# Moving seven weight slots to four addresses modulo 256 in a local-attention and SiLU-FFN kernel

## The chip, the cores and the metric

The kernel runs on one core of one Trainium2 chip. The metric is device time in microseconds (us) of one execution, here the median of three runs. The engines are TensorE (matmuls, PE in the profile; its weight loads are PEld), VectorE (DVE), ScalarE (ACT), GpSimd (POOL), and SyncE (SP), which issues most DMA transfers. SBUF is the on-chip memory with 128 partitions; a tile stands at the same byte address in each partition. PSUM holds the matmuls' sums.

## The reference

A layer norm is followed by two branches on the same normalized input, which are multiplied: dilated local attention with 32 heads of 20, and a SiLU feed-forward network (FFN).

```python
# x: [1, 2048, 640]; wqkv: [640, 1920]; wo: [640, 640]; w1: [640, 1536]; w2: [1536, 640]; all float32
xn = layernorm(x)
q, k, v = split(xn @ wqkv)                        # 32 heads of 20
idx = pos - 2 * arange(8)                         # each position sees 8 earlier ones, 2 apart
attn = softmax(where(idx >= 0, q . k[idx] * 20**-0.5, -1e9))
s = (attn . v[idx]) @ wo
g = silu(silu(xn @ w1) @ w2)
return x + s * g
```

## The kernel before

**Tiling.** The 2048 rows are worked on in four groups of 512 (two halves by two parities of position), and a group in four tiles of 128 rows. For each group there are three kinds of dense work on TensorE, in this order: `qkv_phase` (20 weight units: 4 quarters of the heads by 5 chunks of 128 input channels), from the second group on `wo_phase` for the group before (5 units), and `ffn_phase` (12 units of `w1` and 12 of `w2`, alternating). After the last group `wo_last` closes. Attention itself (scores, softmax, values) runs on VectorE and ScalarE beside the matmuls of the next quarters.

**Three products for one.** Every float32 operand is split into a high and a low half (type float32r), and a product is hi·hi + lo·hi + hi·lo. The activations' halves, transposed, are the tiles `TH[i]` and `TL[i]` (names th and tl in the profile; i is 0 or 1, by group in turn). The hidden layer's halves are `SH[s]` and `SL[s]` (sh and sl; s is the parity of the FFN unit f). A weight unit stands in one of seven ring slots `WR[0]` to `WR[6]` (name w), 5120 bytes per partition: the high half in the first 2560 bytes, the low half in the next. Units take the slots in turn, and a slot is refilled when its unit is done.

**Which operand stands and which moves.** A matmul has a stationary operand, loaded into the array ahead (PEld, 128 columns, 512 bytes per partition), and a moving one that streams through.

| lines | work | stationary | moving | columns | matmuls |
|---|---|---|---|---|---|
| L590 to L592 | qkv | th, tl | w | 480 | 900 |
| L741 to L743 | w1 | w | th, tl | 512 | 720 |
| L624, L626 with sh, sl | w2 | sh, sl | w | 384 and 256 | 576 pairs |
| L624, L626 with th, tl | wo | th, tl | w | 384 and 256 | 240 L624, 225 L626 |
| L542 | first quarter of qkv | th, tl | w | 480 | 60 |

The matmuls of a unit are three per tile and chunk, so on L590 to L592 and on L741 to L743 a block of one unit is 12 and 15 matmuls; on L624 and L626 a `w2` unit is 12 pairs. The order of TensorE's work is written out by hand; a small planner (`Weave`) orders the other engines' work around it by costs and due times. It sees tiles by name, not by address.

**Addresses.** All tiles come from one pool and stand in the order in which the program makes them, rounded up to 32 bytes. All offsets within th, tl, sh, sl and w that the matmuls use are multiples of 256 bytes, so that one number modulo 256 describes each tile.

Of the kernel before, what the change touches and what calls it, by code (L numbers as in the profile page):

```python
# [8 lines left out]
F32 = mybir.dt.float32  # L9
F32R = mybir.dt.float32r  # L10
# [4 lines left out]
P = 128  # L15
S, D, F, H, DH = 2048, 640, 1536, 32, 20
W = 8
DC, FC = D // P, F // P
NQ = 4
HQ = H // NQ  # L20
CQ = HQ * DH
J = 8
T = 4
TOK = T * P
# [5 lines left out]
RING = 7  # L30
# [13 lines left out]
def tsl(t):  # L44
    return slice(t * P, (t + 1) * P)
# [119 lines left out]
def local_attention_silu_ffn(ctx: ExitStack, tc: tile.TileContext, x, wqkv, wo, w1, w2, out):  # L165
    nc = tc.nc
    pool = lambda name, bufs, **kw: ctx.enter_context(tc.tile_pool(name=name, bufs=bufs, **kw))
    sb = pool("sb", 1)
# [16 lines left out]
    def tiles(name, n, shape, dtype=F32):  # L185
        return [sb.tile(shape, dtype, name=f"{name}{i}") for i in range(n)]
# [2 lines left out]
    epst = sb.tile([P, 1], F32, name="epst")  # L189
    MV = sb.tile([P, T, 2], F32, name="mv")  # L190
    ST = [sb.tile([P, 2, 6], F32, name="st0")]
    TH = tiles("th", 2, [P, DC, TOK], F32R)
    TL = tiles("tl", 2, [P, DC, TOK], F32R)
    WR = tiles("w", RING, [P, 2 * D], F32R)
    SH = [None, sb.tile([P, TOK], F32R, name="sh1")]
    SL = [None, sb.tile([P, TOK], F32R, name="sl1")]
    ST.append(sb.tile([P, 2, 6], F32, name="st1"))
    SH[0] = sb.tile([P, TOK], F32R, name="sh0")
    SL[0] = sb.tile([P, TOK], F32R, name="sl0")
    SD = sb.tile([P, 2, T], F32, name="sd")  # L200
    mask = sb.tile([P, T, W], F32, name="mask")
    M = tiles("m", 2, [P, T, HQ])
    Z = tiles("z", 2, [P, 2, T, HQ])
    KV = tiles("kv", NQ, [P, 2, HALO + T, CQ])
    Q = tiles("q", NQ, [P, T, CQ])
# [34 lines left out]
    def dve(n, fn, reads, writes, prio, lock=False):  # L240
        add("DVE", dv(n), fn, reads, writes, prio, lock)

    def act(n, fn, reads, writes, prio, table=None):
        add("ACT", ac(n), fn, reads, writes, prio, table=table)

    def pe(dur, fn, reads, writes):
        add("PE", dur, fn, reads, writes)
        clock[0] += dur
# [44 lines left out]
    for u in units:  # L293
        n = seen[u] = seen.get(u, 0) + 1
# [6 lines left out]
    def width(u):  # L301
        return 3 * CQ if u[0] == "q" else D
# [31 lines left out]
    def w_load():  # L334
# [5 lines left out]
        n = width(u)  # L340
        r = WR[s]
        both = r.rearrange("p (s d) -> p s d", s=2)[:, :, :n]
# [26 lines left out]
    def w_next(*want):  # L369
# [4 lines left out]
        s, n = i % RING, width(want)  # L374
        return WR[s][:, :n], WR[s][:, D:D + n], ("wh", s), ("wl", s)

    def w_done(n=1):
        for _ in range(n):
            w_load()
# [26 lines left out]
    def split_t(src, skeys, c, i):  # L406
# [6 lines left out]
        pe(0.54, turn, skeys, [kp])  # L413
        hi, lo = TH[i][:, c, :], TL[i][:, c, :]
        kh, kl = t_keys(i, [c], kinds=["th"]), t_keys(i, [c], kinds=["tl"])
# [34 lines left out]
    def halo_keys(q):  # L450
        return [("halo", q, 1, 0), ("halo", q, 1, 112), ("halo", q, 2, 0), ("halo", q, 2, 112), ("halo", q, 3, 0),
                ("halo", q, 4, 0)] + [("kv", q, t) for t in range(T)]

    def scores(g, q):
        i = q % 2
        l, e, m, kv, qq = L[i], E[i], M[i], KV[q], Q[q]
        hk = halo_keys(q)
# [51 lines left out]
    def first_quarter(i):  # L509
# [8 lines left out]
        def turn(t):  # L518
# [6 lines left out]
            for a, b, tp, kp in parts:  # L525
                v = tp[:, :(b - a) * P].rearrange("p (c n) -> p c n", n=P)
                act((b - a) * P, lambda a=a, b=b, v=v: nc.scalar.activation(TH[i][:, a:b, tsl(t)], v, AF.Copy),
                    [kp], t_keys(i, range(a, b), [t], ["th"]), 0)
            for a, b, tp, kp in parts:
                v = tp[:, :(b - a) * P].rearrange("p (c n) -> p c n", n=P)  # L530
                dve((b - a) * P, lambda a=a, b=b, v=v: nc.vector.tensor_tensor(
                    out=TL[i][:, a:b, tsl(t)], in0=v, in1=TH[i][:, a:b, tsl(t)].bitcast(F32), op=OP.subtract),
                    [kp] + t_keys(i, range(a, b), [t], ["th"]), t_keys(i, range(a, b), [t], ["tl"]), 0)

        def products(t, part):
            o, kp = ps[t]
            for k in part:
                for c in range(DC):
                    x, kx = (TL, "tl") if k == 1 else (TH, "th")
                    wh, wl, kh, kl = ws[c]  # L540
# [35 lines left out]
    def qkv_phase(g, i, io):  # L576
        for q in range(NQ):
            if g == 0 and q == 0:
                ps = first_quarter(i)
            else:  # L580
                ps = [bank() for t in range(T)]
                for c in range(DC):
                    wh, wl, kh, kl = w_next("q", q, c)
                    for t in range(T):
                        o, kp = ps[t]

                        def unit(c=c, t=t, o=o, wh=wh, wl=wl):
                            o = o[:, :3 * CQ]
                            hi, lo = TH[i][:, c, tsl(t)], TL[i][:, c, tsl(t)]
                            nc.tensor.matmul(o, hi, wh, start=c == 0, stop=False)  # L590
# [17 lines left out]
    def t_keys(i, cs, ts=range(T), kinds=("th", "tl")):  # L608
        return [(k, i, c, t) for k in kinds for c in cs for t in ts]
# [10 lines left out]
    def tm_mm(banks, t, st, w, first, last, cols=(0, 1)):  # L620
        a, b = banks
        h = t % 2
        if 0 in cols:
            nc.tensor.matmul(a[t][0][:, :CA], st, w[:, :CA], start=first, stop=last)  # L624
        if 1 in cols:
            nc.tensor.matmul(b[t // 2][0][:, h * CB:(h + 1) * CB], st, w[:, CA:], start=first and h == 0,  # L626
                             stop=last, skip_group_check=True)
# [14 lines left out]
    def wo_phase(g, i):  # L642
        banks = tm_banks()
        a, b = banks
        for c in range(DC):
            wh, wl, kh, kl = w_next("wo", c)
            for t in range(T):
                def one(c=c, t=t, wh=wh, wl=wl):
                    tm_mm(banks, t, TH[i][:, c, tsl(t)], wh, c == 0, False)
                    tm_mm(banks, t, TH[i][:, c, tsl(t)], wl, False, False)  # L650
                    tm_mm(banks, t, TL[i][:, c, tsl(t)], wh, False, c == DC - 1)
                pe(3 * TM, one, t_keys(i, [c], [t]) + [kh, kl], [a[t][1], b[t // 2][1]])
# [14 lines left out]
    def wo_last(g, i):  # L667
# [22 lines left out]
        def whole(t, cols):  # L690
            for k in range(3):
                for c in range(DC):
                    st = (TH, TH, TL)[k][i][:, c, tsl(t)]
                    tm_mm(banks, t, st, ws[c][k == 1], k + c == 0, k == 2 and c == DC - 1, cols)
# [23 lines left out]
    def ffn_phase(g, i, ix, io):  # L718
        nxt = g + 1 if g + 1 < NG else None
        ps = prev = None  # L720
        for f in range(FC + 1):
# [11 lines left out]
            if f < FC:  # L733
# [11 lines left out]
                w_done()  # L745
                sf, sh, sl = SF[s], SH[s], SL[s]
                act(TOK, lambda sh=sh, h=h: nc.scalar.activation(sh, h, AF.Silu), [kp], [("sh", s)], 0, "silu")  # L747
# [76 lines left out]
```

## Time and profile before

| | |
|---|---|
| three runs | 643.94, 643.47, 643.81 us; median 643.81 |
| the profiled execution's own time | 644.53 us |
| its span, first to last instruction | 642.8 us |
| TensorE busy | 635.4 us, 99% |
| weight loads (PEld) busy | 576.0 us, 90% |
| VectorE, ScalarE, GpSimd busy | 83%, 32%, 20% |
| matmuls | 3502 |

Matmuls overlap in the pipeline and their ends are modelled, so a matmul's duration in the profile says little. What it costs is the time from its start to the start of the next one, which the timeline shows; I call this the spacing.

### The profile page before, as it was taken

Reading aid. Unit: us, or ns where it says so; the run is one execution under the profiler, and the core shown is the slowest. Engines: PE = TensorE matmul, PEld = TensorE weight load, DVE = VectorE, ACT = ScalarE, POOL = GpSimd, SP = SyncE. Lnnn points to the kernel's source line nnn. Section 1 sums busy time; section 2 is a strip of 40 time slices with the busy share of each in tenths; the row PEclk is TensorE's granted clock in tenths of the full one; section 3 lists DMA queues with packets and bytes.
Section 4 is the critical chain, followed back from the end, with each engine's and each line's share of the span. In section 5 each row is a group of like instructions: output and inputs, shape, how many; then the busy total and the mean of one; then the engine's idle time right before and its main releaser. Section 6 shows DMA issues by size and latency. Waiting matters only on the chain.

```text
span 642.8 us, 9033 instructions
## 1 busy us (share of the span) xinstructions
PE 635.4 (99%) x3502; PEld 576.0 (90%) x3502; DVE 536.6 (83%) x532; ACT 206.1 (32%) x401; POOL 126.5 (20%) x171
## 2 busy tenths in 40 slices
PE   7999999999999999999999999999999999999997
PEld 7888899999888999999888999999988899899997
DVE  5699999999999989999939999999106999999714
ACT  5435453453534022324332212223313222233130
POOL 7410000011101241112222125111122213311100
PEclk8999999999999999999999999999999999999999
DMA  9999999777999997656699978965579996876522
GB/s 275 323 309 323 311 403 395 275 226 217 301 319 328 291 306 266 176 184 207 184 257 279 301 215 255 319 180 169 167 203 259 278 293 227 298 258 197 172 83 82
DMA packets 74010, 162.44 MB, mean 253 GB/s; under 512 B 5632, under 2 KB 46816, under 8 KB 73968
## 3 DMA queue, kind: packets, MB, share of 16 engines
q0 software_dynamic: 26672, 82.58, 44.1%
q1 hardware_dynamic: 47296, 79.29, 40.1%
q8 instruction: 27, 0.44, 0.3%
q14 instruction: 15, 0.12, 0.1%
HBM read 109.55 MB, written 34.16 MB: 224 GB/s over the span
## 4 chain that ended last, share of the span: by engine, by line
PE 98%; DMA 1%; DVE 0%; ACT 0%; SPq 0%; issue 0%
PE acc L624 22%; PE acc L626 15%; PE acc L590 10%; PE acc L592 10%; PE acc L591 10%; PE rot L742 9%; PE rot L743 9%; PE rot L741 9%; PE rot L412 2%; PE acc L542 2%; DMA pr<-in_A_wqkv_dram 1%; PE rot L523 0%; PE rot L713 0%; PE acc L515 0%; DVE xin L402 0%; ACT w L355 0%
## 5 line engine op out<-in xcount | busy, mean ns | idle before, releaser
L624 PE MATMUL acc<-w,sh 128*128 128x384 f32 x384 | 114.9, 337 | 0.0
L590 PE MATMUL acc<-w,th 128*128 128x480 f32 x300 | 114.7, 382 | 0.0
L592 PE MATMUL acc<-w,th 128*128 128x480 f32 x300 | 113.5, 378 | 0.0
L591 PE MATMUL acc<-w,tl 128*128 128x480 f32 x300 | 113.4, 378 | 0.0
L626 PE MATMUL acc<-w,sh 128*128 128x256 f32 x384 | 107.2, 279 | 0.0
L460 DVE TENSOR_TENSOR pr<-q,kv 128x2560 f32<-128x2560 f32 x32 | 90.2, 2820 | 11.4 <-DMA kv<-kv 10.9
L741 PE MATMUL rot<-th,w 128*128 128x512 f32 x240 | 94.9, 395 | 0.0
L743 PE MATMUL rot<-th,w 128*128 128x512 f32 x240 | 93.7, 391 | 0.0
L742 PE MATMUL rot<-tl,w 128*128 128x512 f32 x240 | 93.7, 390 | 0.0
L492 DVE TENSOR_TENSOR pr<-e,kv 128x2560 f32<-128x2560 f32 x32 | 90.3, 2821 | 0.7
L463 DVE TENSOR_REDUCE l<-pr 128x128 f32<-128x2560 f32 x32 | 90.0, 2812 | 0.2
L347 POOL DMA_DIRECT2D w<-half_q x52 | 37.5, 721 | 234.3 <-DMA raw<-in_A_wqkv_dram 93.2
L747 ACT ACTIVATE sh<-rot 128x512 fp32r<-128x512 f32 x48 | 28.8, 599 | 159.4 <-PE rot L743 159.3
L497 DVE TENSOR_TENSOR pr<-pr 128x1280 f32<-128x1280 f32 x64 | 76.5, 1195 | 1.1
L347 POOL DMA_DIRECT2D w<-half_w x72 | 38.5, 535 | 181.9 <-PE acc L626 99.2
L626 PEld LDWEIGHTS acc<-w,sh 128*128 128x128 f32 x384 | 72.2, 188 | 1.5
L624 PEld LDWEIGHTS acc<-w,sh 128*128 128x128 f32 x384 | 72.1, 188 | 1.6
L592 PEld LDWEIGHTS acc<-w,th 128*128 128x128 f32 x300 | 56.3, 188 | 8.8
L590 PEld LDWEIGHTS acc<-w,th 128*128 128x128 f32 x300 | 56.3, 188 | 8.3
L591 PEld LDWEIGHTS acc<-w,tl 128*128 128x128 f32 x300 | 56.3, 188 | 8.2
L624 PE MATMUL acc<-w,sl 128*128 128x384 f32 x192 | 58.5, 336 | 0.0
L417 DVE TENSOR_TENSOR tl<-rot,th 128x512 fp32r<-128x512 f32 x35 | 23.9, 682 | 36.4 <-ACT th L416 36.3
(84 smaller groups left out, 1004.8 us busy)
## 6 DMA issues: line engine op xcount, KB each, us to landing
w<-half_w POOLq DMA_DIRECT2D x72, 640.0 KB, 5.6
w<-half_q POOLq DMA_DIRECT2D x52, 480.0 KB, 4.9
half_w<-w SPq DMA_DIRECT2D x24, 640.0 KB
half_q<-w SPq DMA_DIRECT2D x20, 480.0 KB
w<-half_wo POOLq DMA_DIRECT2D x15, 640.0 KB, 4.4
kv<-kv SPq DMA_DIRECT2D x16, 560.0 KB
kv<-kv SPq DMA_DIRECT2D x16, 420.0 KB
gate<-in_B_w_dram SPq DMA_DIRECT2D x16, 320.0 KB
```

What stands on the lines that cost most here:

```text
L460: dve(2560, lambda t=t: nc.vector.tensor_tensor(out=PR, in0=win(qq[:, t:t + 2, :], W, 0), in1=win(kv[:, 0, t:t + 2, :], W, CQ), op=OP.mult ...
L463: dve(2560, lambda t=t: nc.vector.tensor_reduce(out=l[:, t:t + 2].rearrange("p t w h -> p (t w h)"), in_=PR.rearrange("p t w (h d) -> p (t ...
L492: dve(2560, lambda t=t, v=v: nc.vector.tensor_tensor(out=PR.rearrange("p t w (h d) -> p t (w h) d", d=DH), in0=e[:, t:t + 2].rearrange("p ...
L497: dve(2 * n * CQ, lambda n=n: nc.vector.tensor_tensor(out=PR[:, :, 0:n, :], in0=PR[:, :, 0:n, :], in1=PR[:, :, n:2 * n, :], op=OP.add), [] ...
L590: nc.tensor.matmul(o, hi, wh, start=c == 0, stop=False)
L591: nc.tensor.matmul(o, lo, wh, start=False, stop=False)
L592: nc.tensor.matmul(o, hi, wl, start=False, stop=c == DC - 1)
L624: nc.tensor.matmul(a[t][0][:, :CA], st, w[:, :CA], start=first, stop=last)
L626: nc.tensor.matmul(b[t // 2][0][:, h * CB:(h + 1) * CB], st, w[:, CA:], start=first and h == 0, stop=last, skip_group_check=True)
L741: nc.tensor.matmul(h, wh[:, cs], TH[i][:, c, :], start=c == 0, stop=False)
L742: nc.tensor.matmul(h, wh[:, cs], TL[i][:, c, :], start=False, stop=False)
L743: nc.tensor.matmul(h, wl[:, cs], TH[i][:, c, :], start=False, stop=c == DC - 1)
```

## The change

Only the order of the tiles in SBUF changes, and two unused tiles of 64 bytes are added. In the built program the instructions, their order on each engine, their shapes and their waits' order are the same; the addresses differ. Modulo 256 the tiles that TensorE reads stand at:

| tile | before | after |
|---|---|---|
| th0, th1 | 0, 0 | 0, 0 |
| tl0, tl1 | 0, 0 | 0, 128 |
| w0, w1, w2, w3, w4, w5, w6 | 0, 0, 0, 0, 0, 0, 0 | 0, 64, 128, 192, 192, 64, 64 |
| sh0, sl0 | 64, 64 | 64, 64 |
| sh1, sl1 | 0, 0 | 64, 64 |
| ident (transposes) | 128 | 128 |
| xin, o (transposes) | 224, 224 | 96, 96 |

All tiles made after `sd` (z, kv, q, o, pr, l, e, xin, gate, xr, sf, raw) move by the same 128 bytes.

```diff
-    TH = tiles("th", 2, [P, DC, TOK], F32R)
-    TL = tiles("tl", 2, [P, DC, TOK], F32R)
-    WR = tiles("w", RING, [P, 2 * D], F32R)
-    SH = [None, sb.tile([P, TOK], F32R, name="sh1")]
-    SL = [None, sb.tile([P, TOK], F32R, name="sl1")]
-    ST.append(sb.tile([P, 2, 6], F32, name="st1"))
-    SH[0] = sb.tile([P, TOK], F32R, name="sh0")
-    SL[0] = sb.tile([P, TOK], F32R, name="sl0")
+    def apart(n):
+
+        sb.tile([P, n], F32, name=f"apart{len(gaps)}")
+        gaps.append(n)
+
+    gaps = []
+    TH = [sb.tile([P, DC, TOK], F32R, name="th0"), None]
+    TL = [sb.tile([P, DC, TOK], F32R, name="tl0"), None]
+    TH[1] = sb.tile([P, DC, TOK], F32R, name="th1")
+    mask = sb.tile([P, T, W], F32, name="mask")
+    TL[1] = sb.tile([P, DC, TOK], F32R, name="tl1")
+    M = [sb.tile([P, T, HQ], F32, name="m0")]
+    WR = []
+    for k in range(RING):
+        if k == 1:
+            ST.append(sb.tile([P, 2, 6], F32, name="st1"))
+        elif k in (2, 3):
+            apart(16)
+        elif k == 5:
+            M.append(sb.tile([P, T, HQ], F32, name="m1"))
+        WR.append(sb.tile([P, 2 * D], F32R, name=f"w{k}"))
+    SH = tiles("sh", 2, [P, TOK], F32R)
+    SL = tiles("sl", 2, [P, TOK], F32R)
     SD = sb.tile([P, 2, T], F32, name="sd")
-    mask = sb.tile([P, T, W], F32, name="mask")
-    M = tiles("m", 2, [P, T, HQ])
     Z = tiles("z", 2, [P, 2, T, HQ])
```

## The prediction

> **What bounds the kernel.** I read the page first (busy times, granted clock, the chain that ended last), then TensorE's own waits, then the groups by line.
>
> ```profile
> span 642.8 us, 9033 instructions
> ...
> PE 635.4 (99%) x3502; PEld 576.0 (90%) x3502; DVE 536.6 (83%) x532; ACT 206.1 (32%) x401; POOL 126.5 (20%) x171
> ...
> PEclk8999999999999999999999999999999999999999
> ...
> PE 98%; DMA 1%; DVE 0%; ACT 0%; SPq 0%; issue 0%
> ```
>
> ```profile
> PE rot L523 <- DVE xin L402: 2.3, 1, 2.3
> PE rot L515 <- POOL ident masks.py:199: 1.4, 1, 1.4
> ```
>
> The chain that ended last is TensorE for 98% of the span, at full granted clock after the first slice, and TensorE's matmuls wait for others only twice, 3.7 us together, both in the first stage. So the time is the sum of the matmuls' spacings. Any nanosecond that the addresses add to or take from a spacing goes straight into the time; what they do to VectorE, ScalarE or a transfer counts only if TensorE would begin to wait.
>
> The groups give the counts. L591 and L592 have the count of L590, L742 and L743 that of L741.
>
> ```profile
> L624 PE MATMUL acc<-w,sh 128*128 128x384 f32 x384 | 114.9, 337 | 0.0
> L590 PE MATMUL acc<-w,th 128*128 128x480 f32 x300 | 114.7, 382 | 0.0
> L741 PE MATMUL rot<-th,w 128*128 128x512 f32 x240 | 94.9, 395 | 0.0
> L624 PE MATMUL acc<-w,sl 128*128 128x384 f32 x192 | 58.5, 336 | 0.0
> L624 PE MATMUL acc<-w,th 128*128 128x384 f32 x160 | 48.9, 338 | 0.0
> L624 PE MATMUL acc<-w,tl 128*128 128x384 f32 x80 | 25.8, 338 | 0.0
> ```
>
> The spacings come from TensorE's timeline (start, modelled duration, line). Five rows bound four blocks in a row; left out between them are the other matmuls of each block.
>
> ```profile
> 95.72 0.39 PE L741 MATMUL rot<-th,w 128*128 128x512 f32 x1
> ...
> 99.12 0.34 PE L624 MATMUL acc<-w,sh 128*128 128x384 f32 x1
> ...
> 100.28 0.33 PE L624 MATMUL acc<-w,sh 128*128 128x384 f32 x1
> ...
> 102.57 0.40 PE L741 MATMUL rot<-th,w 128*128 128x512 f32 x1
> ...
> 106.02 0.33 PE L624 MATMUL acc<-w,sh 128*128 128x384 f32 x1
> ...
> 109.54 0.60 PE L412 MATMUL rot<-ident,xin 128*128 128x128 f32 x4
> ```
>
> Call the stationary tile's address minus the moving tile's, modulo 256, the distance. The w1 block from 95.72 has 15 matmuls at distance 0: 3.40 us, 226.7 ns each, or 0.4427 ns per column. This is the lowest steady pace I find, and I take it as the pace without stalls. At that pace a pair of 384 and 256 columns takes 283.3 ns and a matmul of 480 columns 212.5 ns.
>
> The w2 block from 99.12 is of sh0 and sl0, at distance 64: 12 pairs in 3.45 us, 287.5 ns each, and from 100.28 on 8 pairs in 2.29 us, 286.2 ns each. The block from 106.02 is of sh1 and sl1, at distance 0: 12 pairs in 3.52 us, 293.3 ns. The two blocks differ in nothing else that the program fixes, so the old layout already holds a trial of the change: distance 64 is worth 5.8 to 7.1 ns per pair. The Trainium skill (TensorE: Matmul & The Clock Gate, Part 2, step on LDWEIGHTS) says the opposite, that loading the next weights takes no read bandwidth from the running matmul; by it these blocks would be alike and the sum of the change nothing. The trace disagrees by those 5.8 ns, in this kernel.
>
> The same rows hold the price. The w1 block after the sh0 block takes 106.02 - 102.57 = 3.45 us, 230.0 ns per matmul, against 226.7 in the block that follows an sh1 block. After a block at another distance the streams need some matmuls to settle; that costs 50 ns per entry here.
>
> The two remaining kinds of work, qkv and wo, all at distance 0:
>
> ```profile
> 56.00 0.38 PE L592 MATMUL acc<-w,th 128*128 128x480 f32 x1
> ...
> 59.90 0.38 PE L592 MATMUL acc<-w,th 128*128 128x480 f32 x1
> ```
>
> ```profile
> 204.45 0.34 PE L624 MATMUL acc<-w,th 128*128 128x384 f32 x1
> ...
> 211.80 0.34 PE L624 MATMUL acc<-w,tl 128*128 128x384 f32 x1
> ```
>
> The first two rows are 18 matmuls apart: 3.90 us, 216.7 ns each, 4.2 over the pace without stalls. The other two are 25 pairs apart: 7.35 us, 294.0 ns, 10.7 over it.
>
> **The change part by part.** Nothing is added or removed on any engine and no wait changes; only distances do. Going through the program's matmuls with the new addresses gives the counts below.
>
> *qkv, 900 matmuls, all at distance 0 now.* After, 132 stay there (w0 with th0, th1 and tl0; w2 with tl1), 280 come to 64, 132 to 128, 356 to 192. Of wo's stall of 10.7 ns per pair, 286.2 - 283.3 = 2.9 ns remain at distance 64, which is 27%. No row shows distances 128 and 192, or 480 columns at any but 0. If 27% of 4.2 ns remain, the gain is 3.0 ns for each of 768: -2.3 us. Bounds: all of the stall goes, -3.2 us; or one more stall of the same size comes in its place, +3.2 us. I take -2.3, from the only row with another distance.
>
> *wo, 240 pairs (15 of them, of the last tile, lack the 256-column half).* All but 4 leave distance 0. At 294.0 - 286.2 = 7.8 ns for 236 pairs that is -1.8 us; bounds -2.5 us (pace without stalls) and 0.
>
> *w2, 576 pairs.* Half stand at distance 0 now, the sh1 blocks. After, sh and sl are all at 64, and so are w1, w5 and w6, which serve half of the w2 units: 288 pairs at distance 0 again, and 96, 144 and 48 at 64, 128 and 192. So this part moves its stalls without removing them. The 192 pairs at 128 and 192 have no row: between 0 and 5.8 ns each more than at 64, 0 to +1.1 us. I take +0.3.
>
> *w1, 720 matmuls.* They run without steady stalls now, so here the change can only cost. 600 leave distance 0. If w1 gets qkv's stall there, 4.2 ns each, that is +2.5 us; if the streams settle into a pace without stalls as they do now, nothing. What is sure to change is the entries: 24 of the 48 blocks follow an sh0 block now. I take half of the other 24 to pay 50 ns: +0.6 us.
>
> *Entries to qkv and wo units.* Each unit is in another slot, and so mostly at another distance than the one before: 75 qkv units after the first quarter and 20 units of wo in the loops. At 50 ns each this is +4.75 us, at none 0. In the trace a change of distance is paid by w1 blocks, while the sh0 block itself, entered from w1, averages only 1.3 ns per pair over its later pace, 16 ns in all. I take 10 ns each: +0.95 us, as some neighbours share a distance.
>
> *Everything else.* The weights are moved by DMA into slots that now start at 64 or 192. A load has much time:
>
> ```profile
> w<-half_w POOLq DMA_DIRECT2D x72, 640.0 KB, 5.6
> ```
>
> ```profile
> 309.95 0.71 POOL L347 DMA_DIRECT2D w<-half_q  x1 [1.89 <-PE acc L592]
> ...
> 325.55 0.71 POOL L347 DMA_DIRECT2D w<-half_q  x1 [1.89 <-PE acc L592]
> ```
>
> These issues are six apart, one per slot that comes free every 2.60 us, and the slot is read again six units later, so 5.6 us stand against some 15. A load would have to take nearly three times as long before TensorE waits; then each us beyond that is lost on each unit. The tiles of VectorE and ScalarE move by the same 128 bytes among themselves, and both have idle time. I cost both at nothing. The first quarter's 60 matmuls on L542 I leave as they are.
>
> *Sum.* -2.3 - 1.8 + 0.3 + 0.6 + 0.95 = -2.25 us. The profiled execution took 644.53 us (1.7 of it around its span), so 642.3; it lies 0.7 us above the median of the runs, 643.81, and on that scale the forecast is 641.6 us.
>
> **The rivals.** *Slower: entries eat the gain.* If every change of slot costs what w1 pays after sh0, 50 ns, then 95 entries of qkv and wo and 24 of w1 cost 5.95 us, and with w2's 1.1 against the gains of 4.1 the time is 643.81 + 2.95 = 646.8 us. It decides from (4.1 - 0.3) / 119 = 32 ns per entry. For it speaks that qkv units last only 12 matmuls, fewer than the block of 15 in which w1 paid; against it the cheap entry into the sh0 block.
>
> *No change worth measuring.* Either the sh0 and sh1 blocks differ for another reason than the distance, which is the skill's rule at work, and the time stays at 643.8; or gains and entries cancel. The alternation of the blocks with sh's parity speaks against the first.
>
> *Full relief.* Only distance 0 stalls, and entries cost nothing: -3.2 for qkv, -2.5 for wo, and w2's 288 other pairs lose their 2.9 ns, -0.8: 643.81 - 6.5 = 637.3 us. Against it: distance 64 did not free the sh0 block fully.
>
> **How the numbers follow.** A measurement of this kernel can tell about 0.2%, 1.3 us, from no change. Forecast (a partial gain between 1.3 and 4.5 us): 0.40. Full relief, or near it: 0.14. No change within 1.3 us: 0.20. Slower: 0.26, all of it from costs without a row (128 and 192, and w1 off distance 0). So faster 0.54, same 0.20, slower 0.26. The likeliest case's own range is 639.3 to 642.5 us. The range that should hold 8 times in 10 goes on one side to near full relief, 637.8, and on the other to near the slower rival, 646.2.
>
> **What would show it.** In the profile after: qkv spacings of 213 to 215 ns in units of w1, w3 to w6, and 216.7 still in w0; wo pairs near 287 ns; w2 blocks near 293 ns in w1, w5 and w6 and near 287 in w0, whatever sh's parity; w1 spacings of 226.7 ns late in each block with longer ones early. Wrong would be: qkv staying at 216.7 at distances other than 0 (then its stall is not one of addresses), w1 blocks that stay above 230 ns throughout, or new waits of PE for DMA.

## The result and the profile after

The changed kernel takes 648.05 us (median of four runs, 647.77 to 648.38) against 643.78 us for the kernel before (643.47 to 643.94), a ratio of 1.0067 with a 95% interval of 1.005 to 1.0085. It is slower by 4.3 us. The forecast was 641.6 us: the sign was wrong, and the time lies 1.9 us above the range.

The page of the kernel after, its span, busy times, granted clock and chain:

```profile
span 646.6 us, 9033 instructions
...
PE 639.1 (99%) x3502; PEld 576.4 (89%) x3502; DVE 539.5 (83%) x532; ACT 206.0 (32%) x401; POOL 125.6 (19%) x171
...
PEclk9999999999999999999999999999999999999999
...
PE 92%; DMA 3%; DVE 2%; ACT 1%; SPq 1%; issue 1%; ACTq 0%
...
w<-half_w POOLq DMA_DIRECT2D x72, 640.0 KB, 5.5
```

TensorE's own waits in the kernel after:

```profile
PE rot L536 <- DVE xin L415: 1.5, 1, 1.5
PE rot L528 <- POOL ident masks.py:199: 1.4, 1, 1.4
PE acc L555 <- ACT w L368: 0.5, 1, 0.5
PE acc L639 <- ACT q L439: 0.3, 1, 0.3
```

The instruction counts and the landing time of the weights (5.5 us, before 5.6) have not moved; the granted clock differs only in the first of the 40 slices (9 tenths, before 8), and TensorE waits 3.7 us for others, as before. The chain has only 92% of TensorE in it because it leaves TensorE at the last of these waits, 0.3 us long; nothing more hangs on that. So the added 3.8 us of span are in the spacings of matmuls that wait for nobody. The groups by line (13 lines further down than before) show it faintly, since a modelled duration carries only part of a spacing:

```profile
L637 PE MATMUL acc<-w,sh 128*128 128x384 f32 x384 | 115.6, 338 | 0.0
L603 PE MATMUL acc<-w,th 128*128 128x480 f32 x300 | 115.2, 384 | 0.0
L754 PE MATMUL rot<-th,w 128*128 128x512 f32 x240 | 95.7, 399 | 0.0
```

For the spacings themselves I took the starts of all 3502 matmuls of both traces in program order and summed the differences by kind. After minus before, in us: qkv +0.59 without its first 100 matmuls, w1 +2.13, w2 +1.25, wo +0.44, the first 100 matmuls of qkv (the first quarter's 60 and the next 40) +0.59, the transposes -1.16 (most of it the wait for `xin`, 2.3 us before and 1.5 now). That is +3.84 us, the whole difference of the spans, 3.8. The last two terms are the start of the program, where a new wait for `w` (0.5 us) and the clock of the first slice play in; I read nothing about addresses from them. No kind of the steady work gained anything.

The timeline of the kernel after (start, modelled duration, line). Each pair of rows bounds one block; left out are the other matmuls of the block:

```profile
67.73 0.39 PE L754 MATMUL rot<-th,w 128*128 128x512 f32 x1
...
71.14 0.33 PE L637 MATMUL acc<-w,sh 128*128 128x384 f32 x1
...
88.72 0.40 PE L754 MATMUL rot<-th,w 128*128 128x512 f32 x1
...
92.22 0.34 PE L637 MATMUL acc<-w,sh 128*128 128x384 f32 x1
...
95.82 0.40 PE L754 MATMUL rot<-th,w 128*128 128x512 f32 x1
...
143.48 0.34 PE L637 MATMUL acc<-w,sh 128*128 128x384 f32 x1
...
146.93 0.34 PE L637 MATMUL acc<-w,sh 128*128 128x384 f32 x1
```

The first block is of w1 units in slot w0, at distance 0: 15 matmuls in 3.41 us, 227.3 ns each, about as before (226.7). The second is in w6, at distance 64: 3.50 us, 233.3 ns. The third and the fourth are w2 units, both of slot w0 at distance 64. One takes 3.60 us for 12 pairs, 300.0 ns; the other 3.45 us, 287.5 ns. Same slot, same distance, and two paces. The two read sh1 and sh0, but that is not it: over the four groups of the program the w2 block of slot w0 with sh1 takes 300, 287, 300 and 287 ns per pair. The two at 287 are in the groups that read th1 and tl1; tl1 stands at 128, so the w1 block just ahead of them has other distances in it. And two neighbouring qkv units, in w2 at distance 128 and then in w3 at distance 64:

```profile
53.78 0.38 PE L603 MATMUL acc<-w,th 128*128 128x480 f32 x1
...
56.42 0.38 PE L603 MATMUL acc<-w,th 128*128 128x480 f32 x1
...
59.02 0.38 PE L603 MATMUL acc<-w,th 128*128 128x480 f32 x1
```

They take 2.64 and 2.60 us for 12 matmuls: 220.0 and 216.7 ns, where distance 0 had 216.7. Distance 64 helps qkv by no more than these rows can show, whose starts are given to 10 ns.

### The profile page after: what moved, and what is told of

It reads as the page before. It is cut to its first block, busy times and chain, and to the rows that moved or that the text cites. A ratio compares the mean times of both kernels' runs of the same rounds, so it can differ in the third digit from the quotient of the medians.

```text
span 646.6 us, 9033 instructions
## 1 busy us (share of the span) xinstructions
PE 639.1 (99%) x3502; PEld 576.4 (89%) x3502; DVE 539.5 (83%) x532; ACT 206.0 (32%) x401; POOL 125.6 (19%) x171
## 4 chain that ended last, share of the span: by engine, by line
PE 92%; DMA 3%; DVE 2%; ACT 1%; SPq 1%; issue 1%; ACTq 0%
PE acc L637 22%; PE acc L639 15%; PE rot L756 9%; PE rot L754 9%; PE rot L755 9%; PE acc L603 8%; PE acc L605 8%; PE acc L604 8%; PE rot L425 2%; PE acc L555 2%; DMA raw<-in_A_wo_dram 2%; DVE pr L505 1%; DMA xin<-in_A_x_dram 1%; SPq L450 1%; DVE pr L510 0%
## 5 line engine op out<-in xcount | busy, mean ns | idle before, releaser
L473 DVE TENSOR_TENSOR pr<-q,kv 128x2560 f32<-128x2560 f32 x32 | 91.6, 2864 | 11.0 <-DMA kv<-kv 10.6
L510 DVE TENSOR_TENSOR pr<-pr 128x1280 f32<-128x1280 f32 x64 | 77.9, 1217 | 1.1
```

The source lines that it names most:

```text
L473: dve(2560, lambda t=t: nc.vector.tensor_tensor(out=PR, in0=win(qq[:, t:t + 2, :], W, 0), in1=win(kv[:, 0, t:t + 2, :], W, CQ), op=OP.mult ...
L510: dve(2 * n * CQ, lambda n=n: nc.vector.tensor_tensor(out=PR[:, :, 0:n, :], in0=PR[:, :, 0:n, :], in1=PR[:, :, n:2 * n, :], op=OP.add), [] ...
```

## The experiments

Three theories stood at the start. The first is the prediction's slower rival: each change of distance, from slot to slot or into a w1 block, costs a time of its own. The second: the distances that the slots were moved to are slower in themselves, for as long as a block lasts. The third: the tiles behind `sd`, which moved by 128 bytes, disturb VectorE, ScalarE or a transfer. Each kernel differs from the kernel before in addresses alone, by the order of the tiles and by unused gaps, unless it is told otherwise. Times are medians, ratios stand against the kernel before on the same chip, and changes by kind are sums of spacings of the profiled execution against the profile before. They leave out the transposes and the first 100 matmuls of qkv, which move by up to 1.8 us from profile to profile.

**sh and sl all at distance 64.** The part of the change that the old trace had a row for, alone:

```diff
-    SH = [None, sb.tile([P, TOK], F32R, name="sh1")]
-    SL = [None, sb.tile([P, TOK], F32R, name="sl1")]
     ST.append(sb.tile([P, 2, 6], F32, name="st1"))
-    SH[0] = sb.tile([P, TOK], F32R, name="sh0")
-    SL[0] = sb.tile([P, TOK], F32R, name="sl0")
+    SH = tiles("sh", 2, [P, TOK], F32R)
+    SL = tiles("sl", 2, [P, TOK], F32R)
```

> Layout of before, with sh1 and sl1 moved to 64 beside sh0 and sl0; th, tl and w stay at 0. So every w2 pair stands at distance 64 and nothing else changes. Theory D (the spacing of a matmul follows from its own distance, whatever came before): the 288 pairs of sh1 go from 293.3 to 286.5 ns, -1.9 us, about 641.9. Theory E (a change of distance between blocks costs an entry): the same gain, but the 24 w1 blocks that followed an sh1 block now pay 50 ns each as well, +1.2 us, about 643.1; w1 spacings then average 230 ns in all 48 blocks. Theory M (TensorE's operands do not matter; the loss came from the tiles that were moved beside them): 643.8, nothing but sh1 and sl1 has moved.

Measured: 643.32 against 643.96 us, ratio 0.9988 (0.9978 to 0.9997). w2 gains 1.2 us and w1 pays 0.53 us. A w1 block behind one of the moved sh1 blocks:

```profile
81.29 0.40 PE L739 MATMUL rot<-th,w 128*128 128x512 f32 x1
...
84.74 0.34 PE L622 MATMUL acc<-w,sh 128*128 128x384 f32 x1
```

It takes 3.45 us. By the unrounded starts such blocks go from 226.9 to 229.7 ns per matmul, 42 ns each. That happens in nine blocks, not in 24: the first two w1 blocks of a group have no w2 block just ahead of them, and those in the stretches with transposes move by 21 ns at most. Away from the transposes, both prices read from the old trace held for this shape and this distance.

**All slots at 64,** sh and sl at 128, so that w1 and w2 stand at 64 and qkv and wo at 192, and no slot differs from another:

```diff
-    WR = tiles("w", RING, [P, 2 * D], F32R)
...
     ST.append(sb.tile([P, 2, 6], F32, name="st1"))
...
+    WR = tiles("w", RING, [P, 2 * D], F32R)
+    sb.tile([P, 16], F32, name="gap6")
+    SH = tiles("sh", 2, [P, TOK], F32R)
+    SL = tiles("sl", 2, [P, TOK], F32R)
+    sb.tile([P, 48], F32, name="gap7")
```

> All seven w slots at 64, all of sh and sl at 128, th and tl at 0, the other tiles where before has them. Distances are the same in every unit: w1 64, qkv and wo 192, w2 64. In the changed kernel w1 at 64 had 232.7 ns and qkv at 192 had 218.2 ns. Theory D: the same here, w1 +4.6 ns x 720 = +3.3 us, qkv +1.4 x 860 = +1.2 us, w2 -1.9 us as all pairs stand at 64: about 646.4. Theory E: with one distance for each kind the streams settle; w1 near 227 to 230 ns, qkv at 216.7, w2 287: 642 to 643. Theory M: 643.8.

Measured: 653.23 against 643.96 us, ratio 1.0145 (1.013 to 1.016): w1 +3.59, w2 +4.4, qkv +1.33, wo -0.1 us. It is the slowest kernel of all, though it has no change of distance between slots; the theory of entries cannot explain it. Its timeline, a w1 block and the w2 block behind it, and in the latter two pairs of 384 and 256 columns:

```profile
82.02 0.40 PE L741 MATMUL rot<-th,w 128*128 128x512 f32 x1
...
85.52 0.34 PE L624 MATMUL acc<-w,sh 128*128 128x384 f32 x1
...
87.31 0.34 PE L624 MATMUL acc<-w,sh 128*128 128x384 f32 x1
87.49 0.28 PE L626 MATMUL acc<-w,sh 128*128 128x256 f32 x1
87.61 0.34 PE L624 MATMUL acc<-w,sh 128*128 128x384 f32 x1
87.79 0.28 PE L626 MATMUL acc<-w,sh 128*128 128x256 f32 x1
87.91 0.34 PE L624 MATMUL acc<-w,sl 128*128 128x384 f32 x1
...
89.11 0.40 PE L741 MATMUL rot<-th,w 128*128 128x512 f32 x1
```

The w1 block takes 3.50 us, 233.3 ns per matmul, to its end: it does not settle. The w2 block takes 3.59 us, 299.2 ns per pair, in a fixed pattern of 0.18 and 0.12 us.

**The slots of the changed kernel alone,** with tl1, sh1 and sl1 at 0 and sh0 and sl0 at 64 as before:

```diff
-    WR = tiles("w", RING, [P, 2 * D], F32R)
+    WR = []
+    WR.append(sb.tile([P, 2 * D], F32R, name="w0"))
+    ST.append(sb.tile([P, 2, 6], F32, name="st1"))
+    WR.append(sb.tile([P, 2 * D], F32R, name="w1"))
+    sb.tile([P, 16], F32, name="gap1")
+    WR.append(sb.tile([P, 2 * D], F32R, name="w2"))
...
```

> The weight slots alone: w0 to w6 at 0, 64, 128, 192, 192, 64, 64 as in the changed kernel, everything else at before's addresses modulo 256 (tl1 at 0, sh1 and sl1 at 0, sh0 and sl0 at 64, the other tiles unmoved). Theories D and E: most of the loss of 4.3 us is here, 646.5 to 648.5, with w1 at 231 to 233 ns. Theory M: 643.8, as the tiles of VectorE and the rest stand where before has them.

Measured: 649.2 against 643.96 us, ratio 1.0076 (1.0059 to 1.0093); w1 +2.41, w2 +1.46, qkv +0.63, wo +0.74 us. The slots alone cost 5.2 us, more than the whole change.

**The tiles behind `sd` alone,** moved by a gap of 128 bytes:

```diff
     SL[0] = sb.tile([P, TOK], F32R, name="sl0")
+    sb.tile([P, 32], F32, name="gap5")
     SD = sb.tile([P, 2, T], F32, name="sd")
```

> Layout of before with one unused tile of 128 bytes ahead of sd: all tiles from sd on (xin, o, kv, q, pr and the others) stand 128 bytes further, as in the changed kernel; th, tl, w, sh, sl unmoved. Theories D and E: 643.8, within 0.5, spacings of qkv, w1, w2 and wo as before; the transposes of xin and o are the only matmuls whose distance changes (15 us in all). Theory M: most of the loss, 646 to 648.

Measured: 643.89 against 643.96 us, ratio 1.0003 (0.9994 to 1.0013). They cost nothing in all, as the prediction had it; the third theory falls. By kind w1 is 0.48 us longer and w2 0.28 us shorter, nearly all of it in blocks around the transposes of `xin` and `o`, the only matmuls whose distance this gap changes: ten w1 blocks pay 37 to 43 ns each. So a change of some tenths of a us in a kind need not come from that kind's own distances.

**th, tl, w, sh and sl all moved by 64,** so that every distance between them stays:

```diff
     ST = [sb.tile([P, 2, 6], F32, name="st0")]
+    ST.append(sb.tile([P, 2, 6], F32, name="st1"))
     TH = tiles("th", 2, [P, DC, TOK], F32R)
...
-    ST.append(sb.tile([P, 2, 6], F32, name="st1"))
+    sb.tile([P, 16], F32, name="gap10")
...
```

> All of th, tl, w, sh and sl stand 64 bytes further than in before (th, tl, w, sh1, sl1 at 64, sh0 and sl0 at 128), the other tiles where before has them. Every distance is that of before. Theory R (only the relation of the two operands counts, distance by distance and kind by kind): 643.8 within 0.5, qkv 216.7, w1 226.7 late in each block, w2 286 and 293. Theory A (a moving or stationary tile off a multiple of 256 is slower as such, which e2 could also mean, where w2 at distance 64 took 300 ns with w at 64): slow like the layout with all slots at 64, 648 to 653.

Measured: 644.14 against 643.9 us, ratio 1.0009 (0.9999 to 1.0019), every kind within 0.2 us. At this shift the address itself does not count, only the relation of the two tiles. The ten executions lie between 643.63 and 645.93 us, though, and the profiled one is the shortest; what lengthened others is open.

**All slots at 128,** sh and sl at 192: w1, qkv and wo stand at 128, w2 at 64.

```diff
     TL = tiles("tl", 2, [P, DC, TOK], F32R)
+    mask = sb.tile([P, T, W], F32, name="mask")
     WR = tiles("w", RING, [P, 2 * D], F32R)
...
-    mask = sb.tile([P, T, W], F32, name="mask")
```

> All seven slots at 128, sh and sl at 192, th and tl at 0. Distances everywhere: w1 128, qkv and wo 128, w2 64. Theory R, with the paces that the changed kernel shows per distance: w1 233.4 (+3.8 us), qkv 219.5 (+2.3 us), wo either 287 (-1.5 us) or 300 ns per pair (+1.5 us), w2 at 64 either 287 (-1.9 us) or, as in the layout with all slots at 64, 300 (+4 us): 646.5 to 655. Theory A: as with all slots at 64, 653.

Measured: 651.49 against 643.9 us, ratio 1.0118 (1.0103 to 1.0134): w1 +2.83, w2 +3.06, qkv +2.07, wo -0.9 us. Its timeline, a w2 block and the w1 block behind it, a qkv unit, a wo unit, and the w2 block of the same slot in the second group:

```profile
78.72 0.34 PE L622 MATMUL acc<-w,sh 128*128 128x384 f32 x1
...
82.17 0.39 PE L739 MATMUL rot<-th,w 128*128 128x512 f32 x1
...
85.66 0.34 PE L622 MATMUL acc<-w,sh 128*128 128x384 f32 x1
...
183.17 0.38 PE L588 MATMUL acc<-w,th 128*128 128x480 f32 x1
...
185.81 0.38 PE L588 MATMUL acc<-w,th 128*128 128x480 f32 x1
...
209.17 0.33 PE L622 MATMUL acc<-w,th 128*128 128x384 f32 x1
...
212.61 0.33 PE L622 MATMUL acc<-w,th 128*128 128x384 f32 x1
...
236.96 0.34 PE L622 MATMUL acc<-w,sh 128*128 128x384 f32 x1
...
240.55 0.39 PE L739 MATMUL rot<-th,w 128*128 128x512 f32 x1
```

w1 takes 232.7 ns (3.49 / 15), qkv 220.0 (2.64 / 12), a wo pair 286.7 (3.44 / 12). So distance 128 frees wo of 7 ns and costs qkv 3 and w1 6. The w2 block takes 3.45 us in the first group and 3.59 in the second, 287.5 and 299.2 ns per pair, with the same slot, the same sh1 and sl1 and all distances alike. So it is with the first six w2 blocks of each group: 287 to 288 ns in the first group, 299 to 300 in the other three, and the w1 blocks between them take 232 ns in all four.

**All slots at 192,** sh and sl at 0: w1 stands at 192, qkv, wo and w2 at 64.

```diff
-    WR = tiles("w", RING, [P, 2 * D], F32R)
...
+    mask = sb.tile([P, T, W], F32, name="mask")
     ST.append(sb.tile([P, 2, 6], F32, name="st1"))
...
+    WR = tiles("w", RING, [P, 2 * D], F32R)
+    sb.tile([P, 16], F32, name="gap8")
+    SH = tiles("sh", 2, [P, TOK], F32R)
+    SL = tiles("sl", 2, [P, TOK], F32R)
...
```

> All seven slots at 192, sh and sl at 0, th and tl at 0. Distances everywhere: w1 192, qkv and wo 64, w2 64. Theory R: w1 229.5 (+1.0 us), qkv 216.2 (-0.5 us), wo at 64 and w2 at 64 each either 287 or 300 ns per pair: 641 if both are low, 650 if both are high. Theory A: as with all slots at 64, 653.

Measured: 645.0 against 643.9 us, ratio 1.0018 (1.0008 to 1.0027): qkv -0.6, wo -1.6, w1 +1.86, w2 +0.86 us. Its timeline, four blocks in a row, w2, w1, w2, w1; in the third also a pair:

```profile
72.67 0.34 PE L624 MATMUL acc<-w,sh 128*128 128x384 f32 x1
...
76.26 0.40 PE L741 MATMUL rot<-th,w 128*128 128x512 f32 x1
...
79.75 0.34 PE L624 MATMUL acc<-w,sh 128*128 128x384 f32 x1
...
81.48 0.33 PE L624 MATMUL acc<-w,sh 128*128 128x384 f32 x1
81.65 0.28 PE L626 MATMUL acc<-w,sh 128*128 128x256 f32 x1
81.77 0.33 PE L624 MATMUL acc<-w,sh 128*128 128x384 f32 x1
...
83.20 0.39 PE L741 MATMUL rot<-th,w 128*128 128x512 f32 x1
...
86.65 0.34 PE L624 MATMUL acc<-w,sh 128*128 128x384 f32 x1
```

The w2 block takes 3.59 us, then 3.45; the w1 block 3.49, then 3.45. The distances are the same, yet w2 runs at 299.2 and 287.5 ns per pair and w1 at 232.7 and 230.0 ns, and they change over from block to block. It is not a matter of the single tiles either: the block of sh0 and slot w6 takes 299 ns per pair in the first group of the program and 287 in the second and third. The faster w2 block has 0.17 and 0.12 us where the slow one above had 0.18 and 0.12. So an entry has no fixed price at these distances. What fits is that what came before decides which of two steady patterns the block stays in: the last w2 block of a group follows a w2 block directly, and in the first three groups it keeps the pattern of that block from its first pair on (300 after 299, 287 after 287). No run varied this alone. Whether the patterns are the same in each execution is not shown either: the ten executions lie between 643.69 and 646.40 us, and the profiled one took 646.28.

**sh and sl all at 128,** everything else at 0 (`mask`, then sh and sl, made ahead of st1):

> th, tl and w at 0 as in before, all of sh and sl at 128: w2 at distance 128, w1, qkv and wo at 0. In the changed kernel w2 at 128 shows two paces, 287.5 ns (169 and 119) and 300 ns (181 and 119). Theory R: 287.5 gives -1.9 us against before, 300 gives +5.3 us; w1 blocks pay an entry of up to 50 ns as they do after blocks at 64, +1.2 us at most. So 642 to 643.1 or 649 to 650. Theory A (w off 0 is what costs): sh off 0 is free, 642 to 643.

Measured: 644.46 against 643.9 us, ratio 1.0008 (0.9998 to 1.0018). w2 gains 0.76 us and settles at 287 ns per pair after its first pairs; w1 pays 1.56 us, blocks of 231.3 ns.

**A version from what was found.** In the runs so far qkv was fastest at 64, w2 at 64 when entered from w1 at 0, and w1 at 0. The qkv units do not fill their slot halves, so they can start 192 bytes into them (48 elements), while w1 and w2 units keep the slot's address; sh and sl are all at 64 as in the first experiment:

```diff
...
-        both = r.rearrange("p (s d) -> p s d", s=2)[:, :, :n]
+        o = 48 if u[0] == "q" else 0
+        both = r.rearrange("p (s d) -> p s d", s=2)[:, :, o:o + n]
...
-        return WR[s][:, :n], WR[s][:, D:D + n], ("wh", s), ("wl", s)
+        o = 48 if want[0] == "q" else 0
+        return WR[s][:, o:o + n], WR[s][:, D + o:D + o + n], ("wh", s), ("wl", s)
```

> The layout with all of sh and sl at 64, and besides qkv's weight units placed 48 elements (192 bytes) into their slot and half slot, which they do not fill (480 of 640 columns). So qkv stands at distance 64, w2 at 64, w1 and wo at 0: for each kind the cheapest distance that the runs so far show and that the space allows. Theory R (pace by kind and distance): qkv 215.8 instead of 216.7 ns, -0.8 us, on top of the -0.6 of the layout with sh at 64: about 642.5. If an entry into qkv units or a start off 256 bytes costs, 643.2 or more.

Measured: 642.47 us (642.12 to 643.04) against 643.93, ratio 0.9977 (0.9968 to 0.9987): qkv -0.6, w2 -1.24, w1 +0.55 us. It beats the kernel before and the changed one. Its timeline, a qkv unit, a w2 and a w1 block:

```profile
55.87 0.38 PE L590 MATMUL acc<-w,th 128*128 128x480 f32 x1
...
58.46 0.38 PE L590 MATMUL acc<-w,th 128*128 128x480 f32 x1
...
77.39 0.34 PE L624 MATMUL acc<-w,sh 128*128 128x384 f32 x1
...
80.84 0.40 PE L741 MATMUL rot<-th,w 128*128 128x512 f32 x1
...
84.29 0.34 PE L624 MATMUL acc<-w,sh 128*128 128x384 f32 x1
```

215.8 ns per qkv matmul (2.59 / 12), 287.5 per w2 pair (3.45 / 12), 230.0 per w1 matmul (3.45 / 15). The wo units fill their halves and cannot be moved in this way.

**sh and sl all at 0,** so that every distance is 0 (both made ahead of st1):

> Layout of before with sh0 and sl0 moved back to 0: every matmul but the transposes stands at distance 0. Theory R: all 576 pairs of w2 at 293.4 ns, +1.8 us; no w1 block is entered from another distance, w1 226.7 and -0.6 us: about 645.0. If the sh0 and sh1 blocks of before differ for another reason than the distance: 643.9.

Measured: 644.85 against 643.93 us, ratio 1.0019 (1.0009 to 1.0029): w2 +1.24, w1 -0.34 us, the reverse of the move to 64.

**tl1 alone at 128:**

```diff
-    TL = tiles("tl", 2, [P, DC, TOK], F32R)
+    TL = [sb.tile([P, DC, TOK], F32R, name="tl0")]
+    mask = sb.tile([P, T, W], F32, name="mask")
+    TL.append(sb.tile([P, DC, TOK], F32R, name="tl1"))
+    M = [sb.tile([P, T, HQ], F32, name="m0")]
...
```

> Layout of before with tl1 alone at 128, the third piece of the change. In two of the four groups qkv's and wo's lo products and w1's lo products stand at distance 128 between neighbours at 0. Theory R with entries: w1 in those groups slower, up to 232.5 instead of 227 ns in each block as no block can settle, 360 matmuls x 5 ns = +1.8 us; qkv and wo within 0.7 us: 644 to 646. If a mixed triple settles like distance 0: 643.9.

Measured: 646.47 against 643.93 us, ratio 1.0037 (1.0023 to 1.005): w1 +1.53, w2 +0.54, qkv +0.31 us. A sixth of w1's matmuls read this tile; blocks with it run at 229.3 to 233.3 ns where no transposes stand ahead of them. The parts do not add: the slots cost 5.2 us, tl1 2.5, sh and sl bring 0.6, and all together cost 4.3.

**sh and sl all at 32** (a gap of 32 bytes ahead of them):

> th, tl and w at 0, all of sh and sl at 32: w2 at distance 32, the others at 0. If what counts are pieces of 64 bytes, w2 at 32 behaves like distance 0 (293.4 ns, about 645.0 with all blocks alike) or like 64 (287 ns, about 643.3); if the streams shift against each other continuously, w2 comes out between, near 290 ns, about 644.

Measured: 645.74 against 643.93 us, ratio 1.0028 (1.0019 to 1.0037). At 32 a w2 pair takes 293 ns, as at 0; w2 +1.1, w1 +0.74 us. The w1 blocks behind do notice the 32 bytes: 228.9 ns, against 227.0 with all at 0.

**The paces found**, ns per matmul of w1 and qkv and per pair of w2 and wo, in blocks that stay at one distance:

| distance | w1 (512) | qkv (480) | w2, wo (384 + 256) |
|---|---|---|---|
| 0 | 226.7 | 216.7 | 293 to 294 |
| 64 | 233 | 215.8 | 287 or 300 |
| 128 | 232.5 | 220, in some units 218 | 287 or 300 |
| 192 | 230 or 233 | 218.3 | 293.5 |

The two values at 128 for pairs are from wo in the kernel with all slots at 128 (287) and from w2 in the kernel after, where units in w3 take 298 or 287 ns and those in w4 287; wo at 192 is from the kernel with all slots at 64.

With them the kernel after can be counted again. w1: 280, 120 and 200 matmuls leave distance 0 for 64, 128 and 192, so 280 x 6.3 + 120 x 5.8 + 200 x 3.3 to 6.3 = 3.1 to 3.7 us, less up to 20 entries of 50 ns that were paid before: 2.1 to 3.7, measured 2.13. What the moved `xin` and `o` cost w1 (0.48 us where they moved alone) is not in this sum. qkv, without the first 100 matmuls: 280 at 64, 132 at 128 and 328 at 192, so 280 x -0.9 + 132 x 1.3 to 3.3 + 328 x 1.6 = +0.4 to +0.7 us, measured +0.59. The paces are those of the other kernels, so steady distances account for the loss in w1 and qkv, and no price for a change of slot is needed; the range for w1 is too wide to exclude a small one.

## Why the prediction was wrong

**What held.** Order, the sum of TensorE's waits and, behind the first slice, the clock stayed, TensorE bounds, and the time is the sum of its spacings (3.84 us summed, 3.8 us of span). The loads' cover held. The tail tiles cost nothing. The sh0 and sh1 blocks did differ by the distance: all at 0 costs w2 1.24 us, all at 64 brings 1.2. So the Trainium skill's rule (TensorE: Matmul & The Clock Gate, Part 2, step on LDWEIGHTS), that loading the next weights takes no read bandwidth from the running matmul, is not borne out as a rule on time here: 643.32, 644.85 and 653.23 us come from the same instructions with addresses alone changed. What is read against what inside TensorE no run shows.

**The step that failed** is the carrying over of one row. The only sight of another distance was sh0 at 64, with pairs of 384 and 256 columns, 7.8 ns better than 0. The prediction made of it "27% of the stall remains" at any distance other than 0 and for any shape.

- *qkv, -2.3 us, measured +0.59.* At 64 the pace falls by 0.9 ns, not 3.0, and at 128 and 192 it rises. The prediction's own wrong sign, that qkv stays at 216.7 off distance 0, is nearly what came; its reading, that the 4.2 ns is then no matter of addresses, does not hold, since 128 costs 3.3 ns more.
- *wo, -1.8 us, measured +0.44.* At 64 and 128 the gain of 7 ns exists, with all slots alike (-1.6 us at 64). With the slots mixed, the pairs at 64 and 128 average 293 ns, about as before, since part of them run in the second pattern at 300; 96 pairs at 192 gain nothing; and 0.3 us of the sum is TensorE's new wait for `q`.
- *w1, +0.6 us, measured +2.13.* The assumption "the streams settle" holds only at distance 0. At 64 and 128 the block stays at 232.5 to 233 ns throughout. This was named as a sign of error, and its price, +2.5, as a bound; it should have been the likelier end, as 226.7 ns was the best pace in the trace and so could only be left. The entries in this term were miscounted besides: 20 w1 blocks follow an sh0 block, not 24.
- *w2, +0.3 us, measured +1.25.* The bound of 5.8 ns for distances without a row missed that distance 64 itself has a second pattern, 13 ns slower. The old trace did not have it: there w2 is always entered from w1 at 0. Over whole blocks the pairs at 0, 64, 128 and 192 (288, 96, 144 and 48 of them) now average 294.9, 294.3, 291.5 and 293.3 ns, where 0 and 64 had 294.0 and 289.3: 0.26 + 0.48 + 0.32 + 0.19 us.
- *Entries, +0.95 us.* They have no fixed price. After sh at 64, w1 at 0 pays 42 to 50 ns, as read; at other distances a block can stay in one of two patterns, and with it the cost lasts for the whole block. The loops have 15 wo units, not 20, and `wo_last` changes the slot at every pair, which the term left out.

**The rival "slower: entries eat the gain"** had the right sign and 646.8 us, but not the mechanism: with no slot different from another the kernel is slowest (653.23). A "steady pace off distance 0" rival was missing, though its terms stood in the text: qkv +3.2, w1 +2.5, w2 +1.1 us.

**Still open:** which two accesses meet; whether the period is 256 (only steps of 32 and 64 were tried); and what chooses between 287 and 300 ns. A trace shows starts, not reads. VectorE's long multiplications `pr<-q,kv` also average 2864 ns in the kernel after, against 2820 before and 2820 to 2822 in all twelve experiments; the cause is open, and they are off the path.

## What to carry to other kernels

In this kernel, where TensorE runs back to back, the relation of the stationary tile's address to the moving tile's is worth some 3% of a matmul's spacing (226.7 to 233.3 ns), and its best value differs by shape. The best layout tried won 0.2% of the time and the worst lost 1.5%. In a kernel like it, try the relation for each kind of work separately, and look at every block, since a distance can have two paces. One favourable block in a trace prices that shape at that distance with those neighbours; for another shape or distance even the sign can differ, and a kind that already has the best pace seen is likelier to lose.

## What was not expected of the hardware

The same matmuls on the same tiles have two steady paces. In the kernel with all slots at 192, w2 blocks take 299 or 287.5 ns per pair, without a wait or another clock between them, and away from transposes a block keeps the pattern into which it settles. Also not expected: 32 bytes of distance act as 0 does for w2's own pace (293 ns), while 64 acts otherwise; and moving the lower half of the activations alone (tl1) slows whole w1 blocks in which two thirds of the matmuls read tiles that did not move.
